# Attention and two MLPs on one core: VectorE takes over GpSimd's subtractions, ScalarE takes over sums of the first layer, and the planner's model of a shared port is widened

## The chip, the cores and the metric

The kernel runs on one core of a Trainium2 chip. The metric is the device time of one execution in microseconds; shown is the median of three runs. The engines are TensorE (PE, its weight loads PEld), VectorE (DVE), ScalarE (ACT), GpSimd (POOL) and SyncE (SP), which issues most of the DMA transfers.

## The reference, cut to what matters

```python
scores = scale * q @ k.T + bias(pos)       # 2 batches, 8 heads, 576 positions, 64 per head
attn = exp(scores - max); attn /= sum + 1e-9
x = (attn @ v) as 1152 tokens x 512
# first layer:  512 -> 2048 -> 512
h = x @ w_in;  g = s * relu(h)**2 + b;  x = g @ w_out
# second layer: 512 -> 2048 -> 512
h = x @ w_in;  g = h * tanh(softplus(h));  out = g @ w_out
```
The bias of the scores is a small network of relative position (one input, 32 hidden, one output per head). The two layers' weights come as 64-bit floats and are turned into 32-bit ones on the chip.

## The kernel before, in words

Attention runs as 40 units of (two heads, up to 128 rows, one batch): scores on TensorE, bias and minimum on VectorE (`bias_and_max`), exponential on ScalarE, inverse on VectorE, division on GpSimd, transposes on TensorE (`turn`), copies on ScalarE and VectorE (`keep`), and the product with v (`values`).

Both layers run over three blocks j of 384 tokens and sixteen slices f of 128 hidden values: 48 tiles per layer. A tile is called (L, j, f), with L = 0 for the first layer and 1 for the second. `hidden` makes the tile's hidden product in PSUM (`h`, four banks) with twelve matmuls; the engines make the gate g; `high` splits off its upper part `gh` on ScalarE, `low` the rest `gl` = g - gh; `sums` adds the tile's share of the layer's output to PSUM tiles `y` (four banks), first with gh and then with gl. Weights are split in the same way: `widen` (ScalarE, two steps), `join` (VectorE), `high` and `low` of `Weights`.

The gate of the first layer is `relu` (ScalarE) and `square` (VectorE). That of the second is a chain of `least`, `both`, `one`, `times`, `newton`, `gate` on VectorE (lines 806, 813, 823, 826, 829, 832) and `exp`, `log`, `over` on ScalarE (809, 817, 820). Its order is least, exp, both, log, over, one, times, newton, gate, high, low. `low` runs on VectorE in the first layer and in the last two tiles, and on GpSimd in the other 46 tiles of the second layer (`LASTV = 2`).

When a block of the first layer is complete, `scaled_sum` reads each of its four banks, on VectorE, and writes `y32` to SBUF; `high_sum` (ScalarE) and `low_sum` (VectorE) split it into `yh` and `yl`, the second layer's input. A bank is free for the next block after `scaled_sum`. In the second layer, `out_left` (ScalarE) and `out_right` (VectorE) copy a bank's halves to `ob`, and a DMA stores them.

The order on every engine comes from a planner in the kernel (`Plan.run`). Each step is a `Task` with an engine, an assumed duration, a rank, what it waits for (`after`) and what buffers it takes (`Hold`). The planner repeatedly picks the task that can start first, lower rank first among equals, and the instructions are then issued in that order. `Task.port` marks tasks that the model lets run only one at a time, since VectorE and GpSimd share a port: all of GpSimd's, and on VectorE `bias_row` and `join`. `HLEAD` lets a hidden product rank 25 (2.5 tiles) ahead of the tile's sums. The change touches `Weights.low` (151), `Task` (494), `add_w` (749), `scaled_sum` (869), and the loop over tiles (915 on).

Of the kernel before, what the change touches and what calls it, by code (L numbers as in the profile page):

```python
# [21 lines left out]
def attention_bias_then_two_moe(ctx: ExitStack, tc: tile.TileContext, ins, out):  # L22
# [60 lines left out]
    FILL = 4  # L83
    LASTV = 2
    LXRANK = -78
# [5 lines left out]
    PRANK = -66  # L91
    VRANK = 1
    BIG = 3.0e38
    SD = S // DEAL
# [26 lines left out]
    class Weights:  # L121
# [28 lines left out]

        def low(self):
            minus(nc.vector, self.wlo, self.wf.bitcast(F32), self.whi)
            self.put[self.nm] = self.whi, self.wlo
# [342 lines left out]
    class Task:  # L496
        def __init__(self, engine, us, rank, f, args, after, takes, lag, mb):
            self.engine, self.us, self.rank, self.f, self.args = engine, us, rank, f, args
            self.after, self.takes, self.lag, self.mb = list(after), list(takes), lag, mb
            self.start = self.end = None  # L500
            self.behind, self.past = [], []

            self.port = engine == "POOL" or f.__name__ in ("bias_row", "join") and engine == "DVE"

# [246 lines left out]
    def add_w(L, f, nm, at, early):  # L751
# [14 lines left out]
        t = add(*(("ACT", 0.52) if SPLIT["io".index(nm)] == "a" else ("DVE", 0.34)), at + 2, w.high, after=[t, *new], takes=[hw])  # L766
        t = whave[L, f, nm] = add("DVE", 0.6, at + 3, w.low, after=[t])
        hf.users.append(t)
# [99 lines left out]

    def scaled_sum(j, e):
        if e == 0:  # L870
            yh.append(xp.tile([P, KD, TB], F32R, tag="xh", name=f"yh{j}"))
            yl.append(xp.tile([P, KD, TB], F32R, tag="xl", name=f"yl{j}"))
        if j == 0:
            nc.vector.tensor_scalar(bw[:, e : e + 1], py[0, j, e][:, TB : TB + 1], b_sb, None, op0=ALU.mult)
        y = y32[j, e] = gp[0].tile([P, TB], F32, tag="n", name=f"y32_{j}_{e}")
        nc.vector.tensor_scalar(y, py[0, j, e][:, :TB], s_sb, bw[:, e : e + 1], op0=ALU.mult, op1=ALU.add)

# [28 lines left out]
    for n, (L, j, f) in enumerate((L, j, f) for L in range(2) for j in range(NB) for f in range(NF)):  # L906
# [14 lines left out]
        else:  # L921
            hs = [add("PE", 2.08, at - HLEAD, blk.hidden, after=[lasts, wi, *ready[L, j]], takes=[hh])]
        in_turn(hs[0], "h")
# [47 lines left out]
        if f == NF - 1:  # L971
            ready[1, j] = ready.get((1, j), [])
            for e in range(ne):
                if L == 0:
                    hu = Hold("n")
                    t = add("DVE", 0.6 + 0.13 * (j == 0), at + e, scaled_sum, j, e, after=[ys[e], *ready[1, j][-1:]], takes=[hu])
                    ybank[e].users.append(t)
# [59 lines left out]
```

## Time and profile before

| | us |
|---|---|
| median of three runs | 618.46 (618.12 to 619.24) |
| profiled execution, its own time | 619.38 |
| span of the profiled execution | 617.6 |
| TensorE busy | 592.8 (96%) |
| VectorE busy | 470.2 (76%) |
| ScalarE busy | 381.1 (62%) |
| GpSimd busy | 123.4 (20%) |

The span runs from the first to the last instruction; the execution's own time has 1.78 us more around it. The attention fills the first 210 us, the first layer goes to nearly 420, the second to the end. The granted TensorE clock is the full one in every slice up to the last. Busy time of TensorE includes the pipelined ends of matmuls, so what counts is the idle time between them and the pace from tile to tile.

### The profile page before, as it was taken

Reading aid. Unit: us, or ns where it says so; the run is one execution under the profiler, and the core shown is the slowest. Engines: PE = TensorE matmul, PEld = TensorE weight load, DVE = VectorE, ACT = ScalarE, POOL = GpSimd, SP = SyncE. Lnnn points to the kernel's source line nnn. Section 1 sums busy time; section 2 is a strip of 40 time slices with the busy share of each in tenths; the row PEclk is TensorE's granted clock in tenths of the full one; section 3 lists DMA queues with packets and bytes.
Section 4 is the critical chain, followed back from the end, with each engine's and each line's share of the span. In section 5 each row is a group of like instructions: output and inputs, shape, how many; then the busy total and the mean of one; then the engine's idle time right before and its main releaser. Section 6 shows DMA issues by size and latency. Waiting matters only on the chain.

```text
span 617.6 us, 12029 instructions
## 1 busy us (share of the span) xinstructions
PE 592.8 (96%) x4416; PEld 520.7 (84%) x4416; DVE 470.2 (76%) x1048; ACT 381.1 (62%) x797; POOL 123.4 (20%) x183
## 2 busy tenths in 40 slices
PE   3988999999999999999999999999999999999996
PEld 1444687778888999999999999997898789989984
DVE  5999978877896699634223889899888777787885
ACT  3766877778998899623123788754555444545543
POOL 2223335343344000000000000001222212222120
PEclk9999999999999999999999999999999999999999
DMA  5786756646543678700000377420000100010001
GB/s 121 249 250 204 215 155 179 196 131 201 181 142 103 203 227 281 246 1 1 1 0 13 100 244 242 154 69 1 2 0 1 51 2 2 0 52 1 2 1 51
DMA packets 47083, 65.97 MB, mean 107 GB/s; under 512 B 12720, under 2 KB 32304, under 8 KB 47024
## 3 DMA queue, kind: packets, MB, share of 16 engines
q1 hardware_dynamic: 46688, 64.81, 34.2%
q8 instruction: 35, 0.57, 0.4%
q10 hardware_dynamic: 336, 0.39, 0.2%
q14 instruction: 24, 0.20, 0.1%
HBM read 51.93 MB, written 13.25 MB: 106 GB/s over the span
## 4 chain that ended last, share of the span: by engine, by line
PE 78%; DVE 14%; ACT 3%; DMA 2%; issue 2%; POOL 1%; SPq 0%; ACTq 0%; DVEq 0%
PE h L788 29%; PE y L865 28%; PE s L405 6%; PE po L467 6%; DVE r L257 5%; PE pp L446 5%; PE bias L267 3%; DMA rawq<-in_q_dram 2%; DVE s L415 1%; DVE r L829 1%; DVE u L823 1%; PE pr L448 1%; DVE n L826 1%; PE t L369 1%; DVE qk L163 1%
## 5 line engine op out<-in xcount | busy, mean ns | idle before, releaser
L157 POOL TENSOR_TENSOR gl<-n,gh 128x384 fp32r<-128x384 f32 x46 | 47.4, 1031 | 291.2 <-ACT gh L842 291.2
L437 POOL TENSOR_SCALAR e<-e,rs 128x576 f32<-128x576 f32 x72 | 55.9, 788 | 91.4 <-DVE rs L433 45.1
L257 DVE TENSOR_SCALAR r<-lx,bl 128x352 f32<-128x352 f32 (+17 forms) x144 | 66.6, 523 | 2.1 <-PE bias L267 1.7
L801 DVE SCALAR_TENSOR_TENSOR u<-h,u 128x384 f32<-128x384 f32 x48 | 26.6, 555 | 52.9 <-ACT u L798 52.8
L788 PE MATMUL h<-yh,wli 128*128 128x384 f32 x192 | 64.8, 337 | 0.0
L788 PE MATMUL h<-yh,whi 128*128 128x384 f32 x192 | 64.7, 337 | 0.0
L788 PE MATMUL h<-yl,whi 128*128 128x384 f32 x192 | 64.7, 337 | 0.0
L788 PE MATMUL h<-xh,whi 128*128 128x384 f32 x192 | 64.6, 336 | 0.0
L788 PE MATMUL h<-xh,wli 128*128 128x384 f32 x192 | 64.5, 336 | 0.0
L788 PE MATMUL h<-xl,whi 128*128 128x384 f32 x192 | 64.4, 336 | 0.0
L425 ACT ACTIVATE e<-s,mn 128x576 f32<-128x576 f32 x72 | 55.5, 772 | 9.7 <-DVE mn L415 7.0
L798 ACT ACTIVATE u<-h 128x384 f32<-128x384 f32 x48 | 23.3, 487 | 58.6 <-PE h L788 58.6
L415 DVE CUSTOM_DVE_ANT_0 s<-s,nb 128x576 f32<-128x576 f32 x72 | 52.4, 751 | 9.2 <-PE s L405 9.0
L817 ACT ACTIVATE r<-n,two 128x384 f32<-128x384 f32 x48 | 29.5, 614 | 38.9 <-DVE n L813 38.9
L823 DVE SCALAR_TENSOR_TENSOR u<-n,r 128x384 f32<-128x384 f32 x48 | 35.2, 733 | 23.0 <-ACT r L820 23.0
L405 PE MATMUL s<-qk 64*128 64x144 f32 (+1 forms) x640 | 49.6, 294 | 1.1 <-DVE mn L415 0.8
L405 PEld LDWEIGHTS s<-qk 64*128 64x128 f32 (+1 forms) x640 | 40.6, 176 | 10.4 <-issue 5.2
L865 PE MATMUL y<-who,gh 128*128 128x512 f32 x144 | 43.9, 399 | 4.5 <-ACT gh L842 1.6
L809 ACT ACTIVATE u<-u 128x384 f32<-128x384 f32 x48 | 25.0, 521 | 34.1 <-DVE u L806 34.1
L865 PE MATMUL y<-gl,who 128*128 128x384 f32 (+1 forms) x192 | 44.5, 338 | 0.0
L865 PE MATMUL y<-gh,wlo 128*128 128x384 f32 (+1 forms) x192 | 44.4, 337 | 0.0
L865 PE MATMUL y<-gh,who 128*128 128x384 f32 (+1 forms) x192 | 44.3, 337 | 0.0
(89 smaller groups left out, 1412.3 us busy)
## 6 DMA issues: line engine op xcount, KB each, us to landing
rawi<-in_moe_w_in_dram SPq DMA_DIRECT2D x32, 512.0 KB, 4.3
rawo<-in_moe_w_out_dram SPq DMA_DIRECT2D x32, 512.0 KB, 4.4
nbias_d<-bo SPq DMA_DIRECT2D x36, 295.5 KB, 2.9
nb<-nbias_d SPq DMA_DIRECT2D x32, 288.0 KB, 3.8
rawq<-in_q_dram SPq DMA_DIRECT2D x8, 288.0 KB, 5.8
rawk<-in_k_dram SPq DMA_DIRECT2D x8, 288.0 KB, 6.3
out_dram<-ob SPq DMA_DIRECT2D x9, 256.0 KB, 2.0
natv<-in_v_dram SPq DMA_DIRECT2D x16, 128.0 KB, 3.6
```

Source lines behind the costliest of these rows:

```text
L157: engine.tensor_tensor(out, x, y.bitcast(F32), op=ALU.subtract)
L257: engine.tensor_scalar(r, src, bl[:, g : g + 1], 0.0, op0=ALU.add, op1=ALU.max)
L405: nc.tensor.matmul(self.ps[rows, x if self.both else 2 * j + x, o : o + PIECE], st.qk[d, 0, self.q0 : self.q0 + self.w], st.qk[d, 1, c0 : ...
L415: nc.vector.tensor_tensor_reduce(out=self.s[n][:m], in0=self.ps[:m, 2 * n : 2 * n + 2, :HALF], in1=nb[:m].rearrange("p (n j) -> p n j", n= ...
L425: nc.scalar.activation(out=self.e[n][:m], in_=self.s[n][:m].rearrange("p n j -> p (n j)"), func=AF.Exp, bias=self.mn[n][:m], scale=-1.0, a ...
L437: nc.gpsimd.tensor_scalar(self.e[n][:m], self.e[n][:m], self.rs[:m, n : n + 1], 0.0, op0=ALU.mult, op1=ALU.add)
L446: nc.tensor.transpose(self.pp[:, n, c, :m], self.e[n][:m, c * P : c * P + P], ident[:m, :m])
L467: nc.tensor.matmul(self.po[D * j : D * j + D, :w], va[:, c, j, :], p, start=(c == 0), stop=(c == NQ - 1))
L788: nc.tensor.matmul(self.ph, w[:, c * P : (c + 1) * P], x[:, c, :], start=(c == 0 and n == 0), stop=(c == KD - 1 and n == 2),)
L817: nc.scalar.activation(out=self.r, in_=self.n, func=AF.Ln, bias=two)
L823: nc.vector.scalar_tensor_tensor(self.z, self.n, 2.0, self.r, op0=ALU.add, op1=ALU.mult)
L865: nc.tensor.matmul(o, a, c, start=(f == 0 and i == 0), stop=(f == NF - 1 and i == 2))
```

## The change

- The planner's port is widened to every VectorE task that reads SBUF alone (`PORTS`); the attention's own `low`, which reads PSUM, is left out by its name.
- `LASTV` is 48: `low` of all tiles runs on VectorE.
- `SUMS = "vaa"`: `scaled_sum` of blocks 1 and 2 runs on ScalarE, of block 0 on VectorE. Its rank is 20 lower, and up to two sums may be in work before the first one's `low_sum` is through.
- The hidden products of the second layer's first three tiles rank 10 earlier (`LEAD2`), those of its last four 15 earlier (`TAIL`), which makes four tiles.
- `Weights.low` learns to run on GpSimd, but `LOWS` names VectorE everywhere.

```diff
--- before.py
+++ after.py
@@ -81,7 +81,7 @@
     DEAL = 6
     WEARLY = ("i0", "i1", "o0", "i2", "o1", "i3", "o2", "o3")
     FILL = 4
-    LASTV = 2
+    LASTV = 48
     LXRANK = -78
     CUT = 0
     FRANK = 32
@@ -90,6 +90,14 @@
     GRANK = -190
     PRANK = -66
     VRANK = 1
+    PORTS = ("bias_row", "join", "high", "low", "both", "one", "newton", "gate", "low_sum")
+
+    LOWS = ("vv", "vv")
+    LEAD2 = 10
+    SUMS = "vaa"
+    YBUFS = 2
+    YRANK = 20
+    TAIL = 15
     BIG = 3.0e38
     SD = S // DEAL
     scale = 1.0 / float(np.sqrt(D))
@@ -148,8 +156,8 @@
             self.wlo = self.pool[0].tile([P, KD * P], F32R, tag=f"w{self.nm}l", name=f"wl{self.name}")
             copy(SPLIT["io".index(self.nm)], self.whi, self.wf.bitcast(F32))
 
-        def low(self):
-            minus(nc.vector, self.wlo, self.wf.bitcast(F32), self.whi)
+        def low(self, who):
+            minus(nc.gpsimd if who == "p" else nc.vector, self.wlo, self.wf.bitcast(F32), self.whi)
             self.put[self.nm] = self.whi, self.wlo
 
     def minus(engine, out, x, y):
@@ -500,7 +508,7 @@
             self.start = self.end = None
             self.behind, self.past = [], []
 
-            self.port = engine == "POOL" or f.__name__ in ("bias_row", "join") and engine == "DVE"
+            self.port = engine == "POOL" or engine == "DVE" and f.__qualname__.split(".")[-2:] != ["Unit", "low"] and f.__name__ in PORTS
 
     class Hold:
         def __init__(self, what):
@@ -764,7 +772,8 @@
         t = add("DVE", 0.6, at + 1, w.join, after=[t])
         hr.users.append(t)
         t = add(*(("ACT", 0.52) if SPLIT["io".index(nm)] == "a" else ("DVE", 0.34)), at + 2, w.high, after=[t, *new], takes=[hw])
-        t = whave[L, f, nm] = add("DVE", 0.6, at + 3, w.low, after=[t])
+        who = LOWS[L]["io".index(nm)]
+        t = whave[L, f, nm] = add(*(("DVE", 0.6) if who == "v" else ("POOL", 1.3)), at + 3, w.low, who, after=[t])
         hf.users.append(t)
         wused[L, f, nm] = hw.users
 
@@ -866,14 +875,17 @@
 
     py, y32 = {}, {}
 
-    def scaled_sum(j, e):
+    def scaled_sum(j, e, who):
         if e == 0:
             yh.append(xp.tile([P, KD, TB], F32R, tag="xh", name=f"yh{j}"))
             yl.append(xp.tile([P, KD, TB], F32R, tag="xl", name=f"yl{j}"))
         if j == 0:
             nc.vector.tensor_scalar(bw[:, e : e + 1], py[0, j, e][:, TB : TB + 1], b_sb, None, op0=ALU.mult)
         y = y32[j, e] = gp[0].tile([P, TB], F32, tag="n", name=f"y32_{j}_{e}")
-        nc.vector.tensor_scalar(y, py[0, j, e][:, :TB], s_sb, bw[:, e : e + 1], op0=ALU.mult, op1=ALU.add)
+        if who == "a":
+            nc.scalar.activation(out=y, in_=py[0, j, e][:, :TB], func=AF.Identity, scale=s_sb, bias=bw[:, e : e + 1])
+        else:
+            nc.vector.tensor_scalar(y, py[0, j, e][:, :TB], s_sb, bw[:, e : e + 1], op0=ALU.mult, op1=ALU.add)
 
     def high_sum(j, e):
         nc.scalar.activation(out=yh[j][:, e, :], in_=y32[j, e], func=AF.Copy)
@@ -919,7 +931,7 @@
                 hs.append(add("PE", 0.53, 10 * (len(units) + FRANK + 5 * f), blk.hidden, (c,), after=[lasts, wi, *hs, *ready[L, j]],
                               takes=[] if c else [hh]))
         else:
-            hs = [add("PE", 2.08, at - HLEAD, blk.hidden, after=[lasts, wi, *ready[L, j]], takes=[hh])]
+            hs = [add("PE", 2.08, at - HLEAD - (TAIL if n >= 2 * NB * NF - 4 else LEAD2 if NB * NF <= n < NB * NF + 3 else 0), blk.hidden, after=[lasts, wi, *ready[L, j]], takes=[hh])]
         in_turn(hs[0], "h")
         wused[L, f, "i"] += hs
         if not WHOLE:
@@ -973,7 +985,10 @@
             for e in range(ne):
                 if L == 0:
                     hu = Hold("n")
-                    t = add("DVE", 0.6 + 0.13 * (j == 0), at + e, scaled_sum, j, e, after=[ys[e], *ready[1, j][-1:]], takes=[hu])
+                    who = SUMS[j]
+                    before = ready[1, j][-1:] if e < YBUFS else ready[1, j][-YBUFS : len(ready[1, j]) - YBUFS + 1]
+                    t = add(*(("DVE", 0.6 + 0.13 * (j == 0)) if who == "v" else ("ACT", 0.45)), at + e - YRANK, scaled_sum, j, e, who,
+                            after=[ys[e], *(before if YBUFS == 1 or e >= YBUFS else [])], takes=[hu])
                     ybank[e].users.append(t)
                     t = add("ACT", 0.43, at + e, high_sum, j, e, after=[t])
                     t = add("DVE", 0.47, at + e, low_sum, j, e, after=[t])
```

The planner makes a new order of it. Up to the last units of the attention no row differs; from there on the rows move as in these three places. A name ends in the buffer's number; before it stand layer, block and slice where the name has three numbers, block and bank in `y32`, layer, block and bank in `y`, layer and slice in the weights (`wlo`, `who`). Lines of the changed kernel lie 8 or 9 further down.

VectorE where the first layer ends and the second begins, before: sums (`y32_2`) of the last block stand among the last weights and the second layer's first tiles.

```order
L876 TENSOR_SCALAR y32_2_0_5552<-y0_2_0_4731,s_sb_71,bw_73 128x384
L157 TENSOR_TENSOR wlo_1_14_5548<-wfo_1_14_5478,who_1_14_5547 128x512
L832 TENSOR_TENSOR n1_0_1_5500<-n1_0_1_5500,r1_0_1_5505 128x384
L157 TENSOR_TENSOR yl2_5551<-y32_2_0_5552,yh2_5550 128x384
L163 CAST who_1_15_5584<-wfo_1_15_5528 128x512
L806 TENSOR_SCALAR u1_0_3_5588<-h1_0_3_5464 128x384
L157 TENSOR_TENSOR wlo_1_15_5585<-wfo_1_15_5528,who_1_15_5584 128x512
L876 TENSOR_SCALAR y32_2_1_5592<-y0_2_1_4781,s_sb_71,bw_73 128x384
L813 SCALAR_TENSOR_TENSOR n1_0_2_5594<-u1_0_2_5526 128x384
L157 TENSOR_TENSOR yl2_5551<-y32_2_1_5592,yh2_5550 128x384
L876 TENSOR_SCALAR y32_2_2_5605<-y0_2_2_4812,s_sb_71,bw_73 128x384
```

The same place with the change:

```order
L165 TENSOR_TENSOR gl1_0_0_5505<-n1_0_0_5451,gh1_0_0_5504 128x384
L165 TENSOR_TENSOR wlo_1_14_5514<-wfo_1_14_5431,who_1_14_5513 128x512
L832 SCALAR_TENSOR_TENSOR u1_0_1_5460<-n1_0_1_5494,r1_0_1_5497 128x384
L835 SCALAR_TENSOR_TENSOR n1_0_1_5494<-n1_0_1_5494,h1_0_1_5436 128x384
L165 TENSOR_TENSOR yl2_5526<-y32_2_0_5527,yh2_5525 128x384
L838 SCALAR_TENSOR_TENSOR r1_0_1_5497<-u1_0_1_5460,r1_0_1_5497 128x384
L171 CAST who_1_15_5554<-wfo_1_15_5491 128x512
L841 TENSOR_TENSOR n1_0_1_5494<-n1_0_1_5494,r1_0_1_5497 128x384
L165 TENSOR_TENSOR wlo_1_15_5555<-wfo_1_15_5491,who_1_15_5554 128x512
L815 TENSOR_SCALAR u1_0_3_5575<-h1_0_3_5539 128x384
L165 TENSOR_TENSOR gl1_0_1_5560<-n1_0_1_5494,gh1_0_1_5559 128x384
L822 SCALAR_TENSOR_TENSOR n1_0_2_5579<-u1_0_2_5507 128x384
```

The sums have left VectorE, and the low parts `gl1_0_0` and `gl1_0_1` stand there.

ScalarE at the same place, before:

```order
L809 ACTIVATE u1_0_2_5526<-u1_0_2_5526 128x384
L879 ACTIVATE yh2_5550<-y32_2_0_5552 128x384
L842 ACTIVATE gh1_0_1_5581<-n1_0_1_5500 128x384
L809 ACTIVATE u1_0_3_5588<-u1_0_3_5588 128x384
L879 ACTIVATE yh2_5550<-y32_2_1_5592 128x384
L817 ACTIVATE r1_0_2_5601<-n1_0_2_5594,two_74 128x384
L820 ACTIVATE r1_0_2_5601<-r1_0_2_5601 128x384
L879 ACTIVATE yh2_5550<-y32_2_2_5605 128x384
```

With the change:

```order
L818 ACTIVATE u1_0_2_5507<-u1_0_2_5507 128x384
L886 ACTIVATE y32_2_0_5527<-y0_2_0_4726,bw_73,s_sb_71 128x384
L891 ACTIVATE yh2_5525<-y32_2_0_5527 128x384
L851 ACTIVATE gh1_0_1_5559<-n1_0_1_5494 128x384
L818 ACTIVATE u1_0_3_5575<-u1_0_3_5575 128x384
L886 ACTIVATE y32_2_1_5581<-y0_2_1_4733,bw_73,s_sb_71 128x384
L826 ACTIVATE r1_0_2_5583<-n1_0_2_5579,two_74 128x384
L891 ACTIVATE yh2_5525<-y32_2_1_5581 128x384
L829 ACTIVATE r1_0_2_5583<-r1_0_2_5583 128x384
L886 ACTIVATE y32_2_2_5602<-y0_2_2_4740,bw_73,s_sb_71 128x384
```

ScalarE now makes the sums itself, each ahead of its high part; the first stands behind exp of tile 2, the second behind exp of tile 3, the third behind log and over of tile 2.

TensorE at the end of the second layer, where the last hidden product (`h1_2_15`) begins, before:

```order
L865 MATMUL y1_2_0_6814<-who_1_12_5456,gh1_2_12_7245 128x512
L865 MATMUL y1_2_1_6821<-who_1_12_5456,gh1_2_12_7245 128x512
L865 MATMUL y1_2_2_6830<-who_1_12_5456,gh1_2_12_7245 128x512
L865 MATMUL y1_2_0_6814<-wlo_1_12_5457,gh1_2_12_7245 128x512
L865 MATMUL y1_2_1_6821<-wlo_1_12_5457,gh1_2_12_7245 128x512
L865 MATMUL y1_2_2_6830<-wlo_1_12_5457,gh1_2_12_7245 128x512
L788 MATMUL h1_2_15_7266<-yh2_5550,whi_1_15_5311 128x384
```

With the change:

```order
L874 MATMUL y1_2_0_6813<-who_1_11_5362,gh1_2_11_7198 128x512
L874 MATMUL y1_2_1_6820<-who_1_11_5362,gh1_2_11_7198 128x512
L874 MATMUL y1_2_2_6826<-who_1_11_5362,gh1_2_11_7198 128x512
L874 MATMUL y1_2_0_6813<-wlo_1_11_5363,gh1_2_11_7198 128x512
L874 MATMUL y1_2_1_6820<-wlo_1_11_5363,gh1_2_11_7198 128x512
L874 MATMUL y1_2_2_6826<-wlo_1_11_5363,gh1_2_11_7198 128x512
L797 MATMUL h1_2_15_7256<-yh2_5525,whi_1_15_5408 128x384
```

The last hidden product has moved ahead of tile 12's sums: it comes after the first two thirds of tile 11's.

## Rows read from the trace of the kernel before

**Rows 1.** The page, parts 1 and 4: busy time of the engines; the chain by engine.
```profile
PE 592.8 (96%) x4416; PEld 520.7 (84%) x4416; DVE 470.2 (76%) x1048; ACT 381.1 (62%) x797; POOL 123.4 (20%) x183
...
PE 78%; DVE 14%; ACT 3%; DMA 2%; issue 2%; POOL 1%; SPq 0%; ACTq 0%; DVEq 0%
```

**Rows 2.** Stretches: stretch, its us, busy us (instructions) of each engine, PEclk, DMA share, GB/s.
```profile
0.00:120.00 120.00, 104.15 (x1194) 67.38 (x1196) 103.05 (x287) 81.34 (x192) 40.15 (x63) 1.00 0.68 197
...
340.00:400.00 60.00, 60.00 (x346) 59.99 (x345) 51.41 (x94) 47.66 (x92) 0.00 (x0) 1.00 0.60 185
400.00:430.00 30.00, 28.66 (x152) 26.41 (x151) 27.44 (x53) 16.52 (x32) 3.50 (x3) 1.00 0.13 41
430.00:600.00 170.00, 168.47 (x841) 151.51 (x840) 137.44 (x252) 85.44 (x171) 41.92 (x42) 1.00 0.03 10
```

**Rows 3.** Waits of TensorE, whole span: us in total, times, longest.
```profile
PE y L865 <- ACT gh L842: 1.6, 2, 1.0
PE y L865 <- DVE ob L891: 1.5, 1, 1.5
PE y L865 <- DVE y L876: 1.3, 2, 0.9
...
PE pp L446 <- ACT pt L161: 0.4, 1, 0.4
```

**Rows 4.** The chain in order of time, 430 to 450 us: start, us, what.
```profile
440.71 2.10 PE h L788 x12
442.81 2.08 PE y L865 x9
444.90 2.11 PE h L788 x12
```

**Rows 5.** Groups, 205 to 618 us: line, engine, operation, xcount | busy us, mean ns | idle before.
```profile
L157 POOL TENSOR_TENSOR gl<-n,gh 128x384 fp32r<-128x384 f32 x46 | 47.4, 1031 | 291.2 <-ACT gh L842 291.2
...
L823 DVE SCALAR_TENSOR_TENSOR u<-n,r 128x384 f32<-128x384 f32 x48 | 35.2, 733 | 23.0 <-ACT r L820 23.0
...
L829 DVE SCALAR_TENSOR_TENSOR r<-u,r 128x384 f32<-128x384 f32 x48 | 31.8, 663 | 0.0
...
L832 DVE TENSOR_TENSOR n<-n,r 128x384 f32<-128x384 f32 x48 | 26.5, 552 | 0.6
```

**Rows 6.** Timeline of VectorE, 408.6 to 411.1 us: start, us, engine, line, operation.
```profile
409.27 0.55 DVE L829 SCALAR_TENSOR_TENSOR r<-u,r 128x384 f32<-128x384 f32 x1
409.74 0.55 DVE L813 SCALAR_TENSOR_TENSOR n<-u 128x384 f32<-128x384 f32 x1
```

**Rows 7.** Timeline, 417 to 422 us: VectorE's third sum, TensorE's start behind it.
```profile
420.56 0.68 DVE L876 TENSOR_SCALAR y<-y,s_sb,bw 128x384 f32<-128x384 f32 x1
...
421.29 0.50 PE L865 MATMUL y<-who,gh 128*128 128x512 f32 x1 [0.89 <-DVE y L876]
```

**Rows 8.** Timeline of VectorE, 480 to 486 us.
```profile
479.49 0.56 DVE L823 SCALAR_TENSOR_TENSOR u<-n,r 128x384 f32<-128x384 f32 x1 [0.31 <-ACT r L820]
480.09 0.55 DVE L826 SCALAR_TENSOR_TENSOR n<-n,h 128x384 f32<-128x384 f32 x1
480.56 1.24 DVE L829 SCALAR_TENSOR_TENSOR r<-u,r 128x384 f32<-128x384 f32 x1
```

**Rows 9.** Timeline, 603 to 613 us: VectorE, and TensorE's last hidden product and last sums.
```profile
603.61 1.06 DVE L823 SCALAR_TENSOR_TENSOR u<-n,r 128x384 f32<-128x384 f32 x1 [1.09 <-ACT r L820]
...
603.93 0.34 PE L788 MATMUL h<-yh,wli 128*128 128x384 f32 x1
...
611.05 0.50 PE L865 MATMUL y<-who,gh 128*128 128x512 f32 x1 [0.99 <-ACT gh L842]
```

**Rows 10.** Timeline, 193.5 to 199 us: ScalarE's copy, TensorE's transposes.
```profile
196.61 1.01 ACT L161 ACTIVATE pt<-pp 128x1024 f32<-128x1024 f32 x1
...
197.76 1.06 PE L446 MATMUL pp<-ident,e 128*128 128x128 f32 x8 [0.38 <-ACT pt L161]
```

**Rows 11.** Groups of ScalarE by form, up to 205 us.
```profile
L161 ACT ACTIVATE bo<-bias,li 128x384 f32<-128x384 f32 x2 | 1.2, 582 | 1.8 <-PE bias L267 1.8
```

## The prediction

> **What bounds the kernel now.** I read the page first. TensorE is busy 592.8 of 617.6 us and takes 78% of the chain that ended last; VectorE is second in both [rows 1]. The stretches say where TensorE is idle: 15.9 us in the first 120 us, and after that next to nothing until 400 us, then 1.3 us in 400 to 430, 1.5 us in 430 to 600, and the end [rows 2]. The table of waits names what ended the late idle time: high gate parts (1.6 us in two waits), one output copy (1.5 us), first-layer sums (1.3 us in two), and in the attention one wait of 0.4 us [rows 3]. The chain shows the pace between them: a tile's hidden product takes 2.10 us and its product with the second weights 2.08, from one hidden product to the next 4.19, 96 tiles, with no idle time between [rows 4]. So TensorE bounds, and less waiting for the other engines gives time only at these few places: 1.3 us near 420, 1.5 at 485, 1.6 in the tail, 0.4 at 197, 4.8 us in all. This is the ceiling of the gain. The idle time of the first 120 us lies where the order of every engine is unchanged.
>
> **Lower parts to VectorE.** GpSimd's 46 subtractions go (47.4 us, nearly all off the chain), and VectorE gets 46 x 0.552 = 25.4 us [rows 5]; that price is the row of `gate`, a two-input operation of the same shape. VectorE gets something back: `one` (L823) and `newton` (L829) take 0.733 and 0.663 us on average against `gate`'s 0.552, and one of them took 1.24 us beside a GpSimd subtraction [rows 5, 8]. Without that neighbour (0.733 + 0.663 - 2 x 0.552) x 48 = 14.0 us disappear. Net: 11.4 us more in the second layer, 0.24 per tile. From 430 to 600 VectorE was busy 137.4 of 170 us [rows 2]; 40 tiles x 0.24 make it 147, 86%. That is still below TensorE's pace, and what counts is the distance between starts, which for independent neighbours is 0.47 us at a duration of 0.55 [rows 6]: seven operations are 3.3 us of 4.19. I cost this edit at nothing; its cover is 0.9 us per tile. If the cover went, the price would be what the loop lasts beyond 4.19 us, times 46.
>
> The Trainium skill, "VectorE: DVE Perf Modes", section "The DRAIN you can't avoid", says that after every operation the pipeline empties before the next one starts, so that operations should be few; the sum by that is rival (b)'s. The starts of [rows 6] lie closer, so the trace does not agree for independent neighbours.
>
> **First-layer sums on ScalarE, near 420.** TensorE started at 421.29, right after the third sum, which VectorE had begun at 420.56 because it stood behind weights and second-layer operations [rows 7]. The trace has no such sum on ScalarE. From below: its read of a same-shaped bank with one scalar from a column took 0.582 [rows 11], and this one has two; from above, the 0.68 that VectorE needs [rows 7]. I take 0.6, near ScalarE's own row. Now the new order, with 0 where TensorE begins the last first-layer tile's sums; a third of a tile's sums is 0.7. Ahead of that stand hidden products of the second layer's tiles 0, 1, 2, which end at -8.4, -4.9 and -0.7. First sum: behind exp of tile 2, its bank complete at 0.7, so 0.8 to 1.4; TensorE asks at 2.1. VectorE's low part of tile 0: `least` of tile 1 starts at -4.85, and up to the low part come seven operations at 0.47, two casts at 0.34 and two weight steps at 0.60 (distances between starts), so it is done at about 0.95, margin 1.1. Then three hidden products fill TensorE until 9.1. Second sum: behind exp of tile 3 (hidden product ends at 4.9, `least` and exp at 6.1), done at 6.7, asked for at 9.1. Third: behind log of tile 2 and two more, done at 8.8, asked for at 9.8. All arrive 0.7 to 2.4 us early, so the 1.3 us go. For the second token block the sums lie behind two weight steps; by the same count the fourth is done 5.0 us after the start of the block's last sums and asked for at 5.8. For the first block VectorE keeps them, now in pairs, and TensorE no longer has hidden products between their uses: the fourth is done at about 5.6 and asked for at 5.8, a thin margin.
>
> **485 us.** TensorE waited 1.5 us for an output copy [rows 3] that came behind a chain delayed by a `newton` of 1.24 us [rows 8]. In the new order the copy stands behind `least` of the last hidden product (which ends 0.7 before the last sums start), `one`, `times` and a low part: 1.4 us after the start of these sums; copy done at 1.8, asked for at 2.8. The 1.5 us go.
>
> **The tail.** The last tile's chain lasted from about 604.1, where its last hidden product (603.93) lets the next instruction start, to 611.05, so 6.95 us, 0.5 of it behind a `one` of 1.06 us beside GpSimd [rows 9]. TensorE had 0.7 + 2 x 2.1 = 4.9 us of other work after the hidden product, and stood 1.6 us. Now one more tile of sums, 2.1 us, lies there: 7.0 us of work against a chain of some 6.4. The 1.6 us go. What follows the last product (4 us of copies and a store) is the same.
>
> **Attention's end.** Near 197 TensorE waited 0.38 us for a copy of 1.01 us that ScalarE began at 196.61 [rows 10]. Now the last unit's scores stand behind the transposes of an earlier unit, and two weight steps have moved from ahead of four exponentials to ahead of the last two: I take -0.3, with bounds of -0.4 and, if the last exponentials come later by the moved steps, +0.8.
>
> **Sum.** -1.3 - 1.5 - 1.6 - 0.3 = -4.7; I give back 0.4 for the thin margin at the first block and one more such place: -4.3. The profiled execution took 619.38 us, 0.92 above the median of 618.46; on its own scale it becomes 615.1, on the median's 614.2. 0.2%, 1.24 us, is about what a measurement of this kernel can tell from no change.
>
> **The rivals.**
> (a) One wait stays or moves, 0.17. For: the sums' margins hang on ScalarE's order, and one late `least` shifts exp, sum and log together. Against: each margin above. With the 1.5 of 485 or the 1.6 of the tail kept, or new ones up to 2.5: 615.3 to 616.7.
> (b) Each VectorE operation holds the engine for its whole duration, 0.06. With the gap of 0.04 that a dependent pair shows (479.49 + 0.56 to 480.09 [rows 8]) four times, a tile costs 7 x 0.552 + 0.16 = 4.0 us, the slack shrinks to 0.2, and the tail's nine operations end 0.8 us later: the tail's 1.6 stay and about 0.5 elsewhere, 616.3. Against: [rows 6].
> (c) Slower, 0.07: the loop through VectorE and ScalarE becomes longer than a tile. In the second block the low part of tile n-1 stands ahead of `one` of tile n, and waits for ScalarE's high part of n-1. If that comes late, `one` starts 2.7 us after `both` instead of 2.2, and the loop is 4.6 us; it decides from 4.19 on. With 0.4 us over 30 tiles, less 3 us of lead, and 1.6 us of the gains left: 618.5 + 9 - 1.6 = 626. Against: where the low part stands there, ScalarE makes the high part before `over`, and my count of the loop is 4.07; pairs of tiles in the third block count 7.6 of 8.4 us.
> (d) No change, 0.05: in the first layer the hidden products lead by three tiles where it was up to six, and between 340 and 400 us VectorE and ScalarE are busy 51.4 and 47.7 of 60 us [rows 2]; waits of 3 to 5 us there eat the gain: 617.3 to 619.7.
> That the change does not do what it says has little room: the 46 rows are gone from GpSimd's order.
>
> **The numbers.** Forecast 0.65, within 613.3 to 615.3. The range of 613.1 to 616.7 adds (a) and (b): 0.88 less the edges. Faster by over 0.2%: forecast, (a) and (b), 0.88; within 0.2%: (d), 0.05; slower: (c), 0.07.
>
> **What would show it.** No TensorE wait above 0.2 us after 200 us; sums on ScalarE near 0.6 us; `one` and `newton` at 0.55; VectorE about 86% busy from 430 to 600; the last product near 609. It is wrong if the chain after 430 shows VectorE for long stretches, if the pace exceeds 4.19 us a tile, or if TensorE waits between 270 and 400.

## The result, and the profile after

The changed kernel took 612.98 us (median of four runs, 610.9 to 614.03), the kernel before beside it 618.53 (618.12 to 619.24): a ratio of 0.9905 with an interval of 0.9877 to 0.9933. It is faster, as forecast, but by more: 5.5 us by the medians against 4.3, and the median lies 0.1 us below the whole range (613.1 to 616.7). The profiled execution took 614.03 us, its span is 612.2.

The page of the changed kernel, parts 1 and 4, answers to [rows 1]:

```profile
PE 591.0 (97%) x4416; PEld 520.7 (85%) x4416; DVE 475.8 (78%) x1086; ACT 389.0 (64%) x805; POOL 79.5 (13%) x137
...
PE 87%; DVE 6%; DMA 3%; ACT 1%; issue 1%; POOL 0%; SPq 0%; DVEq 0%; ACTq 0%
```

GpSimd lost 44 us, VectorE gained only 5.6, and TensorE's share of the chain rose from 78 to 87%. The stretches of the changed kernel (columns as in [rows 2]):

```profile
340.00:400.00 60.00, 60.00 (x346) 60.00 (x345) 52.49 (x96) 52.70 (x102) 0.00 (x0) 1.00 0.66 202
400.00:430.00 30.00, 30.00 (x164) 28.68 (x163) 25.66 (x53) 18.33 (x36) 0.00 (x0) 1.00 0.06 18
430.00:600.00 170.00, 170.00 (x851) 153.42 (x850) 147.04 (x300) 88.37 (x173) 0.00 (x0) 1.00 0.03 10
```

TensorE is idle nowhere after 205 us (and for 0.1 us from 120 to 205): from 190 us on its table of waits is empty, where the kernel before had the rows of [rows 3]. VectorE is busy 147.04 of 170 us (forecast: 147). Its groups from 205 to 612 us, and ScalarE's new sum from 340 to 430 us (line, engine, operation, count | busy us, mean ns | idle before). The lines of the sums and of the output copies lie 12 further down than before, not 8 or 9: L876 is L888, L891 is L903; ScalarE's sum is L886.

```profile
L841 DVE TENSOR_TENSOR n<-n,r 128x384 f32<-128x384 f32 x48 | 26.7, 557 | 1.1
...
L165 DVE TENSOR_TENSOR gl<-n,gh 128x384 fp32r<-128x384 f32 x48 | 26.6, 555 | 6.8 <-ACT gh L851 6.7
...
L832 DVE SCALAR_TENSOR_TENSOR u<-n,r 128x384 f32<-128x384 f32 x48 | 26.5, 553 | 4.6 <-ACT r L829 4.6
L838 DVE SCALAR_TENSOR_TENSOR r<-u,r 128x384 f32<-128x384 f32 x48 | 26.5, 552 | 0.0
```

```profile
L886 ACT ACTIVATE y<-y,bw,s_sb 128x384 f32<-128x384 f32 x8 | 5.1, 668 | 1.0 <-DVE gl L165 0.7 <-DVE yl L165 0.3
```

`one` (now L832) and `newton` (L838) fell to 0.55 us, the price of `gate`. The sum on ScalarE takes 0.67 us, not 0.6; the margins swallowed it.

**A measure free of the start.** The start of the fifth hidden product differs by over 3 us between executions of one and the same order (run e4_tail_0 below), so times of a single profile say little to a tenth. From that product's start to the end of the last product, two profiles of this order agree within 0.04 us. In the changed kernel these are the rows

```profile
216.77 0.34 PE L797 MATMUL h<-xh,whi 128*128 128x384 f32 x1
...
607.81 0.40 PE L874 MATMUL y<-who,gl 128*128 128x512 f32 x1
```

which make 391.44 us, by ends that have one more digit. The kernel before had 215.93 to 613.54, 397.61 us. So the change gives **6.17 us** there. The five late idle rows of before add up to 4.49 us (0.43, 0.89, 1.53, 0.65, 0.99; [rows 3] has them rounded). The 1.7 us between the two numbers is the question of the experiments: theory A puts it into the price of a wait, theory B into TensorE's pace beside GpSimd, theory C into the sums and their order.

### The profile page after: what moved, and what is told of

Same layout as the page of the kernel before. It is cut to its first block, busy times and chain, and to the rows that moved or that the text cites. A ratio compares the mean times of both kernels' runs of the same rounds, so it can differ in the third digit from the quotient of the medians.

```text
span 612.2 us, 11959 instructions
## 1 busy us (share of the span) xinstructions
PE 591.0 (97%) x4416; PEld 520.7 (85%) x4416; DVE 475.8 (78%) x1086; ACT 389.0 (64%) x805; POOL 79.5 (13%) x137
## 4 chain that ended last, share of the span: by engine, by line
PE 87%; DVE 6%; DMA 3%; ACT 1%; issue 1%; POOL 0%; SPq 0%; DVEq 0%; ACTq 0%
PE y L874 33%; PE h L797 33%; PE po L475 6%; PE s L413 6%; PE pp L454 5%; DVE r L265 4%; PE bias L275 3%; DMA rawq<-in_q_dram 2%; DVE s L423 2%; DMA nb<-nbias_d 1%; PE t L377 1%; PE pr L456 1%; DVE qk L171 0%; ACT e L433 0%; ACT bo L169 0%
## 5 line engine op out<-in xcount | busy, mean ns | idle before, releaser
L445 POOL TENSOR_SCALAR e<-e,rs 128x576 f32<-128x576 f32 x72 | 58.3, 820 | 88.2 <-DVE rs L441 51.5
L874 PE MATMUL y<-who,gl 128*128 128x512 f32 x144 | 43.4, 395 | 0.0
L874 PE MATMUL y<-wlo,gh 128*128 128x512 f32 x144 | 43.2, 395 | 0.0
```

The source lines that it names most:

```text
L445: nc.gpsimd.tensor_scalar(self.e[n][:m], self.e[n][:m], self.rs[:m, n : n + 1], 0.0, op0=ALU.mult, op1=ALU.add)
L874: nc.tensor.matmul(o, a, c, start=(f == 0 and i == 0), stop=(f == NF - 1 and i == 2))
```

## Where a wait's price hides

The timeline of TensorE in the kernel before, at the wait of 485 us (start, duration, line, what; in brackets the idle time before):

```profile
483.52 0.39 PE L865 MATMUL y<-wlo,gh 128*128 128x512 f32 x1
483.74 0.40 PE L865 MATMUL y<-who,gl 128*128 128x512 f32 x1
485.67 0.51 PE L865 MATMUL y<-who,gh 128*128 128x512 f32 x1 [1.53 <-DVE ob L891]
486.02 0.39 PE L865 MATMUL y<-wlo,gh 128*128 128x512 f32 x1
```

In the flow such products start 0.23 us apart, but each is drawn 0.39 to 0.40 long. The idle row counts from 484.14, the drawn end of the last product; in the flow the next one would have started at 483.97. That is 0.17 us more than the row says. The product behind the wait is drawn 0.51 long, and the next starts 0.35 after it instead of 0.23: another 0.12. The Trainium skill, "Perfetto Trace Analysis", section "Tensor Engine Instruction (MATMUL, LD_WEIGHTS)", says that the end of a TensorE instruction in a trace is estimated and not observed; the rows fit that, since the next product starts 0.17 us before the drawn end, though two products that overlap would look the same.

So I summed distances between starts instead of ends, each against the median distance of the same pair of products in the changed kernel. Before, 400 to 440 us had 2.10 us too much where the two idle rows say 1.32, 480 to 500 had 1.87 where the row says 1.53, and the tail 2.11 for 1.64: 6.08 us in all.

Of the 2.10 us, the two waits make 1.87. Most of the rest is a third one that no table of waits lists:

```profile
427.71 0.86 PE L865 MATMUL y<-who,gl 128*128 128x512 f32 x3
428.59 0.44 PE L788 MATMUL h<-yh,whi 128*128 128x384 f32 x1
428.87 0.34 PE L788 MATMUL h<-yl,whi 128*128 128x384 f32 x1
```

The first of these hidden products starts 0.41 us after the third `y` product (428.18) instead of 0.23, and the next 0.28 after it instead of 0.17: 0.29 us lost with an idle row of 0.02 us, too short to be listed.

The run with a wait in nearly every tile tests this, and prices VectorE's slack at once.

**Four times the lower part.**

```diff
-            minus(nc.gpsimd if who == "p" else nc.vector, self.gl[:, :TB], self.g, self.gh[:, :TB])
+            for _ in range(4 if self.L else 1):
+                minus(nc.gpsimd if who == "p" else nc.vector, self.gl[:, :TB], self.g, self.gh[:, :TB])
```

> The changed kernel, in which each second-layer gate's lower part is computed four times into the same buffer: three VectorE operations more per tile. It makes VectorE the bound on purpose and gives TensorE a wait in nearly every tile. 3 x 0.47 = 1.41 us against 0.74 us of idle time: a tile becomes 0.6 to 0.7 us longer, 46 tiles less a lead of some three: 25 to 32 us more, 637 to 645 us. What a wait costs: by theory A the stretch of equal work lengthens by the idle rows plus 0.3 us per wait; by the rival (the idle rows are the whole price, and the 1.5 us that the change gave beyond them come from elsewhere) by the idle rows alone. With one wait per tile that is 0.35 us of idle row against 0.65 us.

It took 685.11 us, a ratio of 1.107 (1.1052 to 1.1089), much more than expected (the next section and the last one say why). TensorE's timeline around two of its waits:

```profile
448.33 0.86 PE L875 MATMUL y<-wlo,gh 128*128 128x512 f32 x3
449.92 0.45 PE L797 MATMUL h<-yh,whi 128*128 128x384 f32 x1 [0.73 <-DVE n L835]
450.20 0.34 PE L797 MATMUL h<-yl,whi 128*128 128x384 f32 x1
...
453.54 0.86 PE L875 MATMUL y<-wlo,gh 128*128 128x512 f32 x3
455.10 0.44 PE L797 MATMUL h<-yh,whi 128*128 128x384 f32 x1 [0.70 <-DVE n L835]
```

From the hidden product at 444.75 to that at 486.14 eight tiles last 41.39 us, 5.17 each; without waits a tile lasts 4.20. The difference is 7.8 us, the eight idle rows (0.69 to 0.76) sum to 5.8: 0.25 us per wait beyond its row, at a granted clock of 1.00. Over the single waits of this run outside the slow-clock stretches named in the last section, 0.40 to 1.58 us long, the distances between starts give 0.25 to 0.29 beyond the row nearly throughout, whatever the length (0.36 once). **A wait costs TensorE its idle row and 0.27 us.** The rival, that the row is the whole price, falls: theory A, with 0.27 for its 0.3.

## How much room VectorE had

**Twice the lower part.** The same edit with 2 in place of 4: one VectorE operation more per tile.

> The changed kernel, in which each second-layer gate's lower part is computed twice into the same buffer: one VectorE operation more per tile, 8 in place of 7. VectorE's idle time in a tile of the changed kernel is 0.65 and 0.09 us. If an operation costs the distance between starts, 0.47 us: 0.27 us are left, TensorE waits nowhere between 430 and 600, and the time is 613 to 614 us (at most 0.5 us more in the tail). If it costs its duration with a gap behind it (8 x 0.552 and four gaps of 0.04 are 4.58 us, 0.39 over a tile's 4.19): TensorE waits in each tile, 628 to 632 us.

628.83 us, a ratio of 1.016 (1.0145 to 1.0175): the number of the second theory, but not its mechanism. VectorE in the changed kernel, one tile of the second block:

```profile
500.30 0.56 DVE L815 TENSOR_SCALAR u<-h 128x384 f32<-128x384 f32 x1
...
502.18 0.55 DVE L841 TENSOR_TENSOR n<-n,r 128x384 f32<-128x384 f32 x1
503.38 0.56 DVE L165 TENSOR_TENSOR gl<-n,gh 128x384 fp32r<-128x384 f32 x1 [0.65 <-ACT gh L851]
503.86 0.55 DVE L832 SCALAR_TENSOR_TENSOR u<-n,r 128x384 f32<-128x384 f32 x1
504.50 0.56 DVE L815 TENSOR_SCALAR u<-h 128x384 f32<-128x384 f32 x1
```

and the same tile with the lower part twice:

```profile
504.55 0.56 DVE L815 TENSOR_SCALAR u<-h 128x384 f32<-128x384 f32 x1
...
506.43 0.55 DVE L841 TENSOR_TENSOR n<-n,r 128x384 f32<-128x384 f32 x1
507.63 1.15 DVE L165 TENSOR_TENSOR gl<-n,gh 128x384 fp32r<-128x384 f32 x2 [0.65 <-ACT gh L851]
508.69 0.55 DVE L832 SCALAR_TENSOR_TENSOR u<-n,r 128x384 f32<-128x384 f32 x1
509.16 0.55 DVE L815 TENSOR_SCALAR u<-h 128x384 f32<-128x384 f32 x1
```

Independent neighbours still start 0.47 us apart at a duration of 0.55. But the 0.65 us before the lower part aren't room: there VectorE waits for ScalarE's upper part of the very tile whose gate it has just made, and the order lets nothing else into that place. They belong to the loop. In the changed kernel the loop is 4.20 us, and only its last step has slack: 0.64 from `one` to `least`, where 0.47 would do. So the spare is 0.17 us a tile, the loop itself 4.03. The second lower part writes the same buffer and starts 0.59 behind the first; 4.03 + 0.59 = 4.62, and the trace has 4.61. With three more it would be 5.80, and in the four-fold run TensorE's waits from 534.88 to 552.25 us end 5.79 apart. My expectations of both runs took the 0.65 for room, and that was wrong.

The Trainium skill, "VectorE: DVE Perf Modes", section "The DRAIN you can't avoid", has the pipeline empty after each operation before the next one starts, and excepts a next operation that is not held; the prediction left out this exception. The traces have both distances: a little over the whole duration, 0.59 at 0.56, where the next operation writes the same buffer (the lower part twice), reads the result (`gate` behind `newton`) or overwrites what the one before reads (`times` behind `one`), and 0.47 elsewhere. What holds the first kind back, the runs do not show.

A long wait brings a second price. In the run with the lower part twice, TensorE waited 4.21 us for an output copy at the end of the second layer's first block. Stretches of that run, and its timeline behind the wait:

```profile
486.00:488.00 2.00, 0.00 (x0) 0.00 (x0) 1.93 (x5) 1.39 (x5) 0.00 (x0) 0.83 0.02 4
488.00:490.00 2.00, 1.62 (x4) 1.34 (x5) 2.00 (x6) 0.04 (x1) 0.00 (x0) 0.50 0.34 131
490.00:494.00 4.00, 4.00 (x12) 3.17 (x11) 3.62 (x7) 1.63 (x4) 0.00 (x0) 0.50 0.34 131
494.00:496.00 2.00, 2.00 (x13) 2.00 (x13) 0.00 (x0) 0.46 (x1) 0.00 (x0) 0.97 0.00 0
```

```profile
488.38 0.80 PE L875 MATMUL y<-who,gh 128*128 128x512 f32 x1 [4.21 <-DVE ob L904]
488.97 0.63 PE L875 MATMUL y<-wlo,gh 128*128 128x512 f32 x1
489.40 0.63 PE L875 MATMUL y<-who,gl 128*128 128x512 f32 x1
```

The granted clock is 0.50, which is 1.2 in place of 2.4 GHz, until 494, and products start 0.43 apart instead of 0.23. That accounts for the run: its measured stretch is 407.29 us, 15.9 more than the changed kernel's; nine idle rows make 10.7, nine times 0.27 is 2.4, a wait at 420 us that leaves no row costs 0.2, and the rest, 2.5, is the slow clock. In the kernel before, the clock stayed at 1.00 through every late wait, so nothing of this was in its 6.17 us.

## Which edit removes which wait

The other ten runs are the kernel before with one or two edits of the change, or the change less one edit. With 0.27 known, their waits should give their times. The table has the ratio to the kernel before, TensorE's late idle rows (after 205 us), these with 0.27 for each, and what the stretch of the trace has beyond the changed kernel's 391.44 us.

| kernel | ratio (interval) | late idle rows, us | with 0.27 each | stretch beyond 391.44 |
|---|---|---|---|---|
| before | 1 | 0.43, 0.89, 1.53, 0.65, 0.99 | 5.84 | 6.17 |
| change | 0.9905 (0.9877 to 0.9933) | none | 0 | 0 |
| e4_tail_0 | 0.9894 (0.9881 to 0.9908) | none | 0 | 0.04 |
| e1_gpsimd_lower | 0.9908 (0.9897 to 0.992) | 0.18 | 0.45 | 0.46 |
| e3_sums_vector | 0.9904 (0.9891 to 0.9916) | none | 0 | 0.19 |
| e2_lower_alone | 0.9944 (0.9929 to 0.9959) | 0.22, 1.15 | 1.91 | 2.16 |
| e5_two_buffers | 0.9995 (0.9984 to 1.0005) | 1.43, 1.28, 0.15, 0.37, 0.98 | 5.56 | 5.50 |
| e6_sums_scalar | 0.9952 (0.9939 to 0.9966) | 0.16, 0.14, 0.64, 0.98 | 3.00 | 2.99 |
| e7_tail_alone | 0.9971 (0.996 to 0.9982) | 0.43, 0.91, 1.56, 0.22 | 4.20 | 4.45 |
| e8_lower_two_buffers | 0.9925 (0.9912 to 0.9937) | 1.23 | 1.50 | 1.44 |
| e11_lower_sums | 0.9905 (0.9888 to 0.9922) | none | 0 | 0.05 |
| e12_sums_tail | 0.9923 (0.9906 to 0.9939) | 0.16, 0.11, 0.20 | 1.28 | 1.27 |

The last two columns agree within 0.33 us. The three widest differences, 0.33, 0.25 and 0.25 us, are those of the kernel before, e7 and e2, and each of these has a wait without a listed row at the first hidden product behind the sums (428.59, 429.26 and 427.74 us), by the distances worth 0.29, 0.29 and 0.23; with these the columns agree within 0.2 us. Nothing is left for a pace that would depend on GpSimd: theory B falls, e1 above all, which has all 42 of GpSimd's subtractions between 430 and 600 us and only 0.46 us more.

**Change less the lower parts.**

```diff
-    LASTV = 48
+    LASTV = 2
```

> The change with the lower parts of 46 second-layer gates back on GpSimd; all else of the change stays. Theory A (the gain is TensorE's waits alone, and each wait costs its idle row plus about 0.3 us: the start-to-start distances of TensorE in the two traces grow by 0.17 more than the idle row at the wait, and by about 0.1 behind it): `newton` and `one` go back to 0.66 and 0.73 us, one to three waits of 0.4 to 1.6 us come back between 430 and 600, matmul pace between them unchanged at 0.175 us a start; 614 to 617 us. Theory B (TensorE itself is slower beside GpSimd's subtractions, and that is the 1.5 us that the five waits leave unexplained): pace of the matmuls from 430 to 600 slower by 0.3% with no wait behind it, about 614.5. Theory C (the lower parts are not what counts, the sums and the order are): 613.

612.39 us. `one` and `newton` went back to 0.66 and 0.63 us between 430 and 600 (the kernel before: 0.75 and 0.68), and still there is no wait there, only 0.18 us at 418 for a sum. This is what theory C forecast (613).

**The lower parts alone**, on the kernel before.

```diff
-    LASTV = 2
+    LASTV = 48
```

> The kernel before with one edit of the change: the lower parts of all second-layer gates on VectorE. The last hidden product moves one tile ahead by this edit alone. Theory A: the waits of 485 and of the tail go (2 x 2 us), the two near 420 stay with 1.3 us of idle rows, 1.9 us by start-to-start distances: 614.5 to 615.5 us, and between 430 and 600 no wait. Theory B: the same pace as in the changed kernel, 613 to 613.5 plus the waits near 420. Theory C: 617 or more, since VectorE, with the sums still on it, is late near 420 for over 3 us.

614.33 us. The waits of 485 and of the tail are gone, and the last hidden product lies one tile ahead by this edit alone. Those near 420 stay (waits of TensorE from 190 us on: total, times, longest):

```profile
PE y L865 <- DVE y L876: 1.4, 2, 1.1
PE pp L446 <- ACT pt L161: 0.4, 1, 0.4
```

**Change with all sums on VectorE.**

```diff
-    SUMS = "vaa"
+    SUMS = "vvv"
```

> The change with all first-layer sums on VectorE again; all else of the change stays. Theory A: the sums stand behind second-layer operations again, one or two waits near 420 with 0.5 to 1.3 us of idle rows and 0.3 more each: 613.5 to 615 us; the first block's end near 270 and the second's near 340 without a wait. Theory C: sums are what counts, so 615 and over. If two buffers for the sums and the lead of the second layer's first tiles carry it: 613, no wait near 420.

611.74 us, no late wait. With the two buffers, the early hidden products and the wider port model in place the sums' engine does not matter: neither A's nor C's number, but the third. Which of the last two it needs beside the buffers was not run; without both, on VectorE, 1.23 us of waiting stay (e8 below).

**Change without the lead of the last four.**

```diff
-    TAIL = 15
+    TAIL = 0
```

> The change with no extra lead for the last four hidden products. The instructions of every engine come out in the changed kernel's order, word for word, so this is the changed kernel once more: it tells that the lead that the change's name speaks of is not made by that line, and it measures how far executions of one program lie apart. All theories: 611 to 614 us, no TensorE wait over 0.2 us after 120 us; the wait for the first natq anywhere from 6.3 to 7.7 us, and the time with it.

610.88 us. It is the changed kernel's order, so the distance to 612.98 is that of executions. In their profiles the fifth hidden product starts at 213.61 and 216.77 us, 3.16 apart. TensorE's first long wait in each, the changed kernel and then this run:

```profile
11.13 0.58 PE L377 MATMUL t<-ident,natq 96*128 96x96 f32 x2 [7.65 <-POOL natq L354]
```

```profile
9.79 1.06 PE L377 MATMUL t<-ident,natq 96*128 96x96 f32 x5 [6.30 <-POOL natq L354]
```

That wait makes 1.35 us of it. Most of the other 1.8 comes at three later waits of the same line of transposes: 0.49, 1.10 and 0.82 us at 26.96, 55.43 and 104.64 us in the changed kernel, where this run has none, 0.61 and 0.06. Why they differ between two executions of one order stays open.

**Single edits on the kernel before**: two buffers and the earlier rank for the sums; the sums on ScalarE; the lead of the last four. All other settings are those of before.

```diff
-    YBUFS = 1
-    YRANK = 0
+    YBUFS = 2
+    YRANK = 20
```

> The kernel before with one edit of the change: first-layer sums ordered ahead by rank 20 and in pairs, still on VectorE. Theory A (waits are removed one by one, each for its idle row plus 0.3 us): the two waits near 420 go (2.1 us by start-to-start distances), those of 485 and of the tail stay (1.85 and 2.1): 616 us. Rival D (one cause, GpSimd's subtractions that slow VectorE's neighbours, stands behind the late waits, so the order alone helps little): 617.5 or more, a wait near 420 stays. Rival E (the late waits sit on the order, and any order that starts the sums earlier moves the others too): 613 to 615, no wait of 1.5 us near 485.

619.19 us, no change. The sums come earlier, but VectorE does them ahead of the second layer's `times` (n L835), and the hidden product behind it waits in their place. Waits of TensorE from 190 us on:

```profile
PE y L874 <- DVE ob L903: 1.4, 2, 1.3
PE h L797 <- DVE n L835: 1.4, 1, 1.4
PE y L874 <- ACT gh L851: 1.4, 2, 1.0
```

```diff
-    SUMS = "vvv"
+    SUMS = "vaa"
```

> The kernel before with one edit of the change: the sums of the first layer's second and third token block on ScalarE. Theory A: the two waits near 420 shrink to at most one of 0.5 us of idle row, the others stay: 616 to 617 us. Rival D: 617.5 or more. Rival E: 613 to 615. The sum on ScalarE lasts about 0.6 us in all of them.

616.3 us. It took away the waits of 420 and with them that of 485, all but 0.16 and 0.14 us. VectorE's timeline ahead of that second place:

```profile
477.17 1.24 DVE L838 SCALAR_TENSOR_TENSOR r<-u,r 128x384 f32<-128x384 f32 x1
...
481.81 0.76 DVE L903 COPY ob<-y 128x256 f32<-128x256 f32 x2
```

and the copy in the kernel before:

```profile
485.19 0.42 DVE L891 COPY ob<-y 128x256 f32<-128x256 f32 x1
```

The `newton` of 1.24 us beside GpSimd, on which I had laid the wait of 485 [rows 8], is still there, and the copy follows it as before: it starts 4.64 us after that `newton` here, 4.63 in the kernel before. What moved is TensorE: the products ahead of its wait end, as drawn, 4.98 us after the start of `newton` here, 3.58 before. So the long `newton` alone doesn't make that wait; it takes the phase between the two queues, and that went with the waits near 420 (both places are clear, or nearly, in e1 and e12 too; both keep a wait in e5 and e7).

```diff
-    TAIL = 0
+    TAIL = 15
```

> The kernel before with one edit of the change: the lead of 15 for the last four hidden products. Here it moves the last hidden products one tile ahead (in the whole change it moves nothing, since the lower parts on VectorE do that already). Theory A: the tail's two waits go (1.6 us of idle rows, 2.1 us by start-to-start distances), those near 420 and 485 stay: 616 us. By the idle rows alone: 616.5 us. Rival D: the last chain is still slow beside GpSimd, a wait of 0.3 to 1 us stays in the tail.

617.75 us. The tail's two waits become one of 0.22: here this line does move the last hidden products one tile ahead. From the end of the last hidden product's work to the end of the last upper part it takes 7.3 us (602.66 to 609.96), and TensorE has 7.0 of other work. A `one` of 1.07 us beside GpSimd stands ahead of that chain, at 599.69; how much of the 0.22 it makes is not shown.

**Pairs of edits on the kernel before**: `LASTV = 48` with the two buffers; `LASTV = 48` with the sums on ScalarE; the sums on ScalarE with the lead of the last four.

> The kernel before with two edits of the change: all gates' lower parts on VectorE, and the first-layer sums in pairs and ahead by rank 20, still on VectorE. Theory A: the waits of 420, 485 and the tail all go, 6 us by start-to-start distances, and with that the two edits give the whole gain of the change: 611 to 613 us. Rival: the sums on ScalarE are needed too, since VectorE has 11 us more work: a wait of 0.5 to 1.2 us near 420, 613 to 614.

614.61 us: the rival. The wait of the hidden product for `times` stays, 1.23 us.

> The kernel before with two edits of the change: all gates' lower parts on VectorE, and the sums of the second and third block on ScalarE. If the late waits are all that counts, each at its idle row plus 0.25 us, and the waits of 420 go with the sums, those of 485 and of the tail with the lower parts: no wait after 200 us, 6.0 us less than before, the ratio 0.990; the order of the attention's end stays, with its wait of 0.38 us. Rival: the two edits disturb one another (VectorE has 0.16 us to spare in a tile once it makes the lower parts): waits of 0.5 to 2 us in the second block, ratio 0.993 to 0.996.

613.34 us beside 619.42 of before: no late wait. These two edits give the whole gain.

> The kernel before with two other edits of the change: the sums of the second and third block on ScalarE, and the lead of 15 for the last four hidden products; the lower parts stay on GpSimd. If the sums alone took both the waits of 420 and of 485 away, and the lead all but 0.2 us of the tail's: three waits of 0.14 to 0.22 us stay, 618.1 - 3.0 - 1.7, a ratio of 0.9925, and moving the lower parts was not needed for the most of the gain. Rival: GpSimd's subtractions make some VectorE operation late again in the new order: a wait of 0.5 to 1.5 us between 430 and 612, ratio 0.994 to 0.997.

614.67 us, as expected, with GpSimd's subtractions left in place. VectorE's groups from 430 to 600 us show that they still cost VectorE time of which TensorE feels little:

```profile
L832 DVE SCALAR_TENSOR_TENSOR u<-n,r 128x384 f32<-128x384 f32 x42 | 34.3, 816 | 24.3 <-ACT r L829 24.3
L838 DVE SCALAR_TENSOR_TENSOR r<-u,r 128x384 f32<-128x384 f32 x42 | 25.4, 605 | 0.0
```

No version beats the change: it, e1, e3, e4 and e11 have intervals that overlap, and in all of them TensorE is without a late wait, or nearly so.

## Why the prediction was right or wrong

**The step that failed** is the size of the three terms, and with them the sentence "this is the ceiling of the gain". The places and the direction were right: all five late waits are gone. But a wait was priced at its idle row: 1.3, 1.5 and 1.6 us measured 2.10, 1.87 and 2.11 by distances between starts. Three places give 6.1, not 4.4 (of the first place's 2.10, about a quarter us is the wait without a listed row); the stretch of the trace has 6.17, and the ratios of the one order (0.9905 and 0.9894) make 5.9 and 6.6 us. The row showed it already: [rows 7] and [rows 9] have products of 0.50 us behind the waits, and I read them only as the time at which TensorE began.

**The 0.4 us given back** for a thin margin were not lost: no wait arose at the first block's end, nor in the first layer, where rival (d) looked for 3 to 5 us.

**The lower parts at nothing**: right in the result, wrong in the cover. Seven distances of 0.47 left 0.9 us of a tile by my working; the trace leaves 0.17, because the loop holds 0.65 us of waiting for ScalarE. The count of 4.07 under rival (c) was the better number (4.03), and I used the other. One more operation per tile would have made rival (c) true: 628.8 us.

**Near 420**: right that the sums on ScalarE end both waits (e6), at 0.67 us each instead of 0.6; the rest of the change without them does it as well (e3). The weights' casts, counted at 0.34 between starts, are 0.38 apart in the trace of before, which the margin of 1.1 us covered.

**485**: right that it goes, wrong in laying it on the `newton` of 1.24 us, which is there in e6 too, beside a wait of 0.14. Three ways end it, or nearly: the lower parts alone, the sums alone (0.14 left), or the change without the lower parts.

**The tail**: it goes, but with hardly any margin: the chain was forecast at 6.4 us against 7.0 of other work, and it did not become shorter. The changed kernel's last chain, from `least` to the products behind it:

```profile
598.57 0.55 DVE L165 TENSOR_TENSOR gl<-n,gh 128x384 fp32r<-128x384 f32 x1
...
599.50 0.55 DVE L815 TENSOR_SCALAR u<-h 128x384 f32<-128x384 f32 x1
...
605.14 0.53 ACT L851 ACTIVATE gh<-n 128x384 fp32r<-128x384 f32 x1 [2.34 <-DVE n L841]
605.70 0.56 DVE L165 TENSOR_TENSOR gl<-n,gh 128x384 fp32r<-128x384 f32 x1 [0.65 <-ACT gh L851]
...
605.75 0.46 PE L874 MATMUL y<-who,gh 128*128 128x512 f32 x1
...
606.31 0.50 PE L874 MATMUL y<-who,gl 128*128 128x512 f32 x1
```

The last hidden product's work ends at 598.77, where the first product behind it starts. The upper part is done at 605.67, 6.9 us later, as in the kernel before (604.11 to 611.00). The 0.5 us behind the long `one` went, but a lower part, now on VectorE, and a `times` (599.03) stand ahead of `least`, which starts 0.73 us after the hidden product's work where it was 0.49, and ScalarE makes an upper part ahead of `log`. TensorE asks for the upper part after 6.98 us (605.75; forecast 7.0), so 0.1 us was left of a margin of 0.6. The product of 606.31 follows the lower part at once, with the 0.50 us of one that has been held. The line meant for the tail, the lead of the last four (`TAIL`), moves nothing in the change (e4): the lead comes from the lower parts.

**Attention's end**: the wait of 0.38 us [rows 10] is gone in the change, e1, e3 and e4 and stays in e2, e5 to e8, e11 and e12. The first group has the wider port model and the earlier hidden products of the second layer's first tiles together; they weren't run apart. Its gain drowns in the 3 us by which the start varies.

**Rivals**: (b) was forecast at 616.3; starts 0.47 us apart between independent neighbours, here as in e9, speak against it. (a), (c) and (d) did not come. The signs named came: no wait after 200 us, `one` and `newton` at 0.55, VectorE 86% busy, the last product's end at 608.2 (forecast: near 609).

## What to carry to other kernels

Price a TensorE wait by the distance between starts, not by the idle row: here each cost 0.27 us more, and over five waits, with one that had no row at all, that hid a quarter of the gain. An engine's room in a loop is not its idle share; first take out the idle time in which it waits, in order, for its own result to come back from another engine. And where several edits remove the same waits, undoing one at a time shows only that each can be spared (e1, e3, e4); making them alone and in pairs shows what suffices. Here two of the change's edits carry the whole gain (e11), and one line does nothing in it (e4).

## What the runs showed that I had not expected

The price of 0.27 us does not depend on the wait's length from 0.11 to 1.6 us; only a second product held in the same place adds about 0.1 (the waits at 485 and at the ends of blocks). Waits up to 1.58 us, one in nearly every tile from 529 to 656 us of the four-fold run, left the granted clock at 1.00. It fell from 1.00 to 0.50 in the wait of 4.21 us, and in the four-fold run four times: at 430.3, behind waits of 1.10 and 1.82 us, until 433.7; at 498.6, behind 1.11 and 1.87, until 512.2; at 662.4, behind 2.69, until 665.8; and at 672.6, behind 1.07, 0.72 and 1.76, to the end. In that run 46 late idle rows make 52.3 us, with 0.27 each 64.7; its stretch is 71.9 us longer than the changed kernel's. The other 7.2 us lie in these four stretches: there the distances between starts, less the rows and 0.27 for each, are too long by some 7 us.
